# A fused retention and gated-MLP kernel: the last 64 rows of both sequences of a pair as one last block, one set of transposed mixing weights, bias rows by DMA

## The chip, the cores and the metric

The kernel runs on one core of one Trainium2 chip. The metric is the time of one execution in device microseconds. The granted clock is the clock that TensorE was given, as a share of its full speed. A run is called slow when it is over 1.5% above the fastest of the same kernel; ratios are taken over fast runs.

## The reference

Eight sequences of 576 rows go through eight heads of retention and then through a gated MLP whose gate mixes rows with a 576 x 576 matrix. Cut to what matters:

```python
# q, k, v: (8, 8, 576, 64) float32
scores = q @ k.transpose(0, 1, 3, 2) / sqrt(64)
Dmat   = where(rel >= 0, gamma[:, None, None] ** rel, 0)      # rel = row - column, one gamma per head
x      = heads side by side of (scores * Dmat) @ v            # (8, 576, 512)

h      = gelu_tanh(x @ w_in)                                  # w_in 512 x 1024
u, v   = h[..., :512], h[..., 512:]
v_n    = (v - mean(v)) / sqrt(var(v) + 1e-6) * g_ln
v_s    = einsum('ts,bsd->btd', w_sg, v_n) + b_sg[None, :, None]   # "token mixing", w_sg 576 x 576
out    = x + (u * v_s) @ w_out                                # float32, (8, 576, 512)
```

## The kernel before

The sequences are taken in four pairs. A pair has 2 x 576 = 1152 rows, which are nine tiles of 128 rows, numbered 0 to 8. Retention works on five blocks of a pair: four full ones of 256 rows, and one half block of 128. The table `RB` names, for each block, its number of tiles, its first tile and the chunks of rows in it as (sequence, row).

```python
RB = [(2, 0, ((0, 0), (0, 128))), (2, 2, ((0, 256), (0, 384))),
      (1, MID, ((0, 512), (1, 0))),                           # MID = 4: the half block is the third
      (2, 5, ((1, 64), (1, 192))), (2, 7, ((1, 320), (1, 448)))]
```

So the middle tile holds rows 512 to 575 of sequence 0 and rows 0 to 63 of sequence 1. In this order the nine tiles are simply 1152 consecutive rows of the output, and each tile of 128 rows is stored as one plain matrix:

```python
outf = out.rearrange("b s d -> (b s) d")
def m_store(i):
    nc.sync.dma_start(outf[128 * i:128 * i + 128, :], cur.pop(("ob", i))[:])
```

Sequence 1 starts in the middle of a tile, so its mixing weights have to be cut at other rows than those of sequence 0. Each sequence has its own five transposed tiles of w_sg, ten in all, 50 transposes on TensorE. Small bias rows are placed into them, and into the tiles `vmid`, by ScalarE:

```python
wT = [[consts.tile([128, S], BF, name=f"wT{e}_{j}") for j in range(SB)] for e in range(2)]
def build_wT(e, j):
    c0 = (64 if e == 0 else 0) + 128 * j
    ...
    for t in range(SB):
        nc.tensor.transpose(tp[:, 128 * t:128 * t + 128], wnat[:, t, c0:c0 + 128], ident[:])
def place_vmid():
    for t in vmid:
        nc.scalar.activation(t[0][NB0:NB0 + 4, :], row4b[:, 0, :F2], Act.Copy)
        nc.scalar.activation(t[1][0:4, :], row4b[:, 0, :F2], Act.Copy)
```

An output tile is `op = uT @ w_out` in PSUM. For the first pair x is added by four more matmuls with the identity and ScalarE evicts; for later pairs a transposing transfer brings x into `xr`, and VectorE adds it at eviction:

```python
def m_X(i):
    ...
    nc.sync.dma_start_transpose(cur["xr", i][:], xTs[p][:, m].rearrange("p j r -> p (j r)"))
def m_Oev(i):
    ...
    if i // NT < XP:                                          # XP = 1: the first pair
        ins = nc.scalar.activation(ob[:], op[:], Act.Copy)
    else:
        ins = nc.vector.tensor_tensor(ob[:], op[:], cur.pop(("xr", i))[:]..., op=Alu.add)
```

For the last block of the last pair, q and k too are transposed by a transfer (`qkT<-qkb` from SBUF to SBUF), not on TensorE. In the profile lines, `pp` are PSUM tiles of the attention, `zd` the products for the retention states, `hv` and `hu` the two halves of x @ w_in, `wp` the token mixing, `op` the output tiles, `qkT` transposed q and k, `xr` transposed x.

All loads, stores and transposing transfers are issued by SyncE into one queue, in the order of a table `ORDER`. The same table holds dummy matmuls (`f9`, `f11`: products into a scratch tile `scr`) that fill gaps of TensorE in the first 45 us.

## Time and profile before

| | kernel before |
|---|---|
| median of 3 runs | 212.21 us (212.01 to 212.43) |
| span of the profiled run, granted clock | 209.1 us, 1.00 |
| TensorE busy | 94% |
| 128x512 output stores (256 KB each) | 36, each of 128 rows of 2 KB |

Here are three further lines of the kernel before: the shares of the chain of work that ended last (fourth part of the page), and, for the line that issues the output stores, the issue times and the time from issue to landing.

```profile
PE 58%; DMA 11%; POOL 9%; SPq 8%; DVE 7%; ACT 3%; issue 2%; DVEq 0%; POOLq 0%; ACTq 0%
```

### The profile page before, as it was taken

What the parts mean: (1) busy time and instruction counts of PE and PEld (TensorE: products, weight loads), DVE (VectorE), ACT (ScalarE), POOL (GpSimd) and SP (SyncE); (2) the same over time, 40 slices, a digit from 0 to 9 for tenths busy, and PEclk for the clock granted to TensorE, in tenths of its full rate; (3) what the DMA queues carried; (4) which work ended last, traced back from release to release, by engine and by line L of the source; (5) the groups of instructions that cost most, each with busy time, mean ns of one, the idle gap of its engine ahead of it and who ended that gap; (6) DMA issues with size and microseconds to landing.
All of it is one profiled execution on the core that took longest, in us unless ns stands there. A gap on an engine that the chain in (4) does not pass through costs nothing.

```text
span 209.1 us, 7861 instructions
## 1 busy us (share of the span) xinstructions
PE 196.8 (94%) x3378; PEld 130.9 (63%) x3378; DVE 152.7 (73%) x293; ACT 119.1 (57%) x198; POOL 113.1 (54%) x157
## 2 busy tenths in 40 slices
PE   7998769999999999999999999999899999999982
PEld 3555456577666768765876676658476657566750
DVE  6876668779949768973994966998677886567463
ACT  3216898894984864469656527575526484534300
POOL 5390369696578788656688498165196070112000
PEclk9999999999999999999999999999999999999999
DMA  6999999999999999999999999998778977255565
GB/s 169 290 334 206 336 262 346 297 298 250 195 270 290 260 261 242 258 252 315 290 264 257 304 264 181 217 213 202 199 205 180 226 107 127 102 154 149 155 201 176
DMA packets 94117, 48.64 MB, mean 233 GB/s; under 512 B 38202, under 2 KB 87362, under 8 KB 94082
## 3 DMA queue, kind: packets, MB, share of 16 engines
q1 hardware_dynamic: 94064, 48.13, 96.5%
q8 instruction: 26, 0.43, 0.9%
q14 instruction: 9, 0.07, 0.2%
q10 hardware_dynamic: 18, 0.00, 0.0%
HBM read 32.79 MB, written 9.44 MB: 202 GB/s over the span
## 4 chain that ended last, share of the span: by engine, by line
PE 58%; DMA 11%; POOL 9%; SPq 8%; DVE 7%; ACT 3%; issue 2%; DVEq 0%; POOLq 0%; ACTq 0%
PE wp L759 15%; PE op L786 10%; PE hv L693 10%; PE hu L740 8%; PE pp L626 5%; DMA uT<-in_moe_w_in_dram 4%; SPq L431 3%; POOL vb L463 3%; POOL qkb L463 3%; PE pp L543 3%; DMA qkT<-qkb 3%; DMA ld<-in_q_dram 2%; PE pp L503 2%; DVE bst L708 2%; DMA xr<-xT 2%
## 5 line engine op out<-in xcount | busy, mean ns | idle before, releaser
L463 POOL TENSOR_TENSOR qkb<-ld,gqv 128x1024 bf16<-128x1024 f32 (+1 forms) x19 | 32.7, 1721 | 22.0 <-DMA ld<-in_q_dram 13.2
L556 DVE TENSOR_TENSOR ret<-pp,msk 128x1024 bf16<-128x1024 f32 x32 | 38.6, 1219 | 5.8 <-PE pp L543 5.5
L759 PE MATMUL wp<-wT,vn 128*128 128x288 bf16 x256 | 40.3, 286 | 0.0
L463 POOL TENSOR_TENSOR vb<-ld,gqv 128x1024 bf16<-128x1024 f32 (+1 forms) x20 | 34.4, 1730 | 8.1 <-DMA ld<-in_v_dram 8.0
L740 PE MATMUL hu<-xT,w_in 128*128 128x256 bf16 (+1 forms) x320 | 37.0, 262 | 1.9 <-ACT xT L682 1.9
L682 ACT ACTIVATE xT<-pp 128x512 bf16<-128x512 f32 (+1 forms) x40 | 24.8, 671 | 23.3 <-PE pp L626 21.5
L693 PE MATMUL hv<-w_in,xT 128*128 128x512 bf16 x144 | 36.2, 380 | 1.6 <-DVE w_in L371 0.9
L769 DVE TENSOR_TENSOR uT<-wp,uT 128x288 bf16<-128x288 f32 x64 | 27.2, 448 | 11.5 <-PE wp L759 11.3
L786 PE MATMUL op<-w_out,uT 128*128 128x512 bf16 x144 | 34.9, 380 | 0.7 <-DVE uT L769 0.6
L708 DVE BATCH_NORM_STATS2 bst<-vg 128x6 f32<-128x512 f32 x36 | 24.7, 685 | 12.1 <-ACT vg L700 12.1
L740 PEld LDWEIGHTS <-w_in 128*128 128x128 bf16 x320 | 27.9, 98 | 8.8 <-issue 2.1
L700 ACT ACTIVATE vg<-hv 128x512 f32<-128x512 f32 x36 | 21.2, 596 | 16.5 <-PE hv L693 11.8
L759 PEld LDWEIGHTS <-vn 128*128 128x128 bf16 x256 | 24.8, 98 | 8.1
L728 ACT ACTIVATE vn<-vg,mv 128x512 bf16<-128x512 f32 x32 | 25.4, 809 | 6.7 <-POOL mv L716 6.6
L750 ACT ACTIVATE uT<-hu 128x512 bf16<-128x512 f32 x36 | 20.9, 595 | 11.4 <-PE hu L740 11.1
L713 POOL TENSOR_SCALAR mv<-mv 128x2 f32<-128x2 f32 (+1 forms) x20 | 4.5, 224 | 41.0 <-DVE mv L709 40.4
L693 PEld LDWEIGHTS <-xT 128*128 128x128 bf16 x144 | 13.2, 98 | 14.2 <-ACT xT L682 1.6
L786 PEld LDWEIGHTS <-uT 128*128 128x128 bf16 x144 | 13.3, 98 | 13.8 <-DVE uT L769 1.0
L802 DVE TENSOR_TENSOR ob<-op,xr 128x512 f32<-128x512 f32 x27 | 17.9, 687 | 5.1 <-PE op L786 5.0
L512 DVE COPY qkT<-pp 128x2048 bf16<-128x2048 bf16 (+1 forms) x15 | 16.6, 1108 | 4.0 <-PE pp L503 4.0
L457 POOL CAST qkb<-ld 128x1024 bf16<-128x1024 f32 (+1 forms) x19 | 18.0, 945 | 2.4 <-DMA ld<-in_k_dram 2.4
L759 PE MATMUL wp<-wT,vmid 128*128 128x288 bf16 x64 | 17.9, 287 | 0.0
(89 smaller groups left out, 234.6 us busy)
## 6 DMA issues: line engine op xcount, KB each, us to landing
out_dram<-ob SPq DMA_DIRECT2D x36, 256.0 KB, 3.6
ld<-in_q_dram SPq DMA_DIRECT2D x16, 512.0 KB, 7.3
ld<-in_k_dram SPq DMA_DIRECT2D x16, 512.0 KB, 6.3
ld<-in_v_dram SPq DMA_DIRECT2D x16, 512.0 KB, 7.1
wst<-in_moe_w_sg_dram SPq DMA_DIRECT2D x2, 576.0 KB, 7.1
wst<-in_moe_w_in_dram SPq DMA_DIRECT2D x1, 1024.0 KB
ld<-in_k_dram SPq DMA_DIRECT2D x8, 128.0 KB, 6.9
ld<-in_q_dram SPq DMA_DIRECT2D x8, 128.0 KB, 6.9
```

The source lines that it names most:

```text
L463: eng.tensor_tensor(dst, src, g.unsqueeze(3).to_broadcast(list(src.shape)), op=Alu.mult)
L556: ins = nc.vector.tensor_tensor(ret[:].rearrange("p r (k t) -> p (r k) t", k=2), sc[:].rearrange("p r (k t) -> p (r k) t", k=2), msk2[:].r ...
L682: nc.scalar.activation(dst, src, Act.Copy)
L693: ins = nc.tensor.matmul(hv[:], xTs[p][:, m, kk, :], w_in[:, kk, F2:], start=(kk == 0), stop=(kk == KK - 1))
L700: unfence(nc.scalar.activation(vgs[i][:], cur.pop(("hv", i))[:], Act.Gelu_apprx_tanh), ("V", i))
L708: nc.vector.bn_stats(bst[:], vgs[i][:])
L728: nc.scalar.activation(vn[:], vg[:], Act.Identity, scale=mv[:, s, 2:3], bias=mv[:, s, 3:4])
L740: ins = nc.tensor.matmul(hu[:, n, :], w_in[:, kk, 128 * c:128 * c + 128], xTs[p][:, m:m + w, kk, :], start=(kk == 0), stop=(kk == KK - 1), ...
L750: unfence(nc.scalar.activation(uTs[p][:, c0:c1, 128 * m:128 * m + 128 * w], cur.pop(("hu", i, half))[:], Act.Gelu_apprx_tanh), ("U", i, half))
L759: ins = nc.tensor.matmul(ps[:], vns[t0 + j][e][:, 128 * c:128 * c + 128], wT[e][j][:, half * HS:(half + 1) * HS], start=(j == 0), stop=(j ...
L769: ins = nc.vector.tensor_tensor(uTs[p][:, c, col:col + HS], cur.pop(("wp", b, c, half))[:], uTs[p][:, c, col:col + HS], op=Alu.mult)
L786: ins = nc.tensor.matmul(op[:], uTs[p][:, c, r], w_out[:, c, :], start=(p >= XP and c == 0), stop=(c == KK - 1), skip_group_check=True)
```

## The change

The intent is to do one thing once instead of twice. If both sequences of a pair are cut at the same rows, they can share one set of mixing weights. The last 64 rows of *both* sequences then form the half block, which comes last in the pair, and all token mixing of the pair follows it. Cuts are marked with "..."; the new order of jobs is left out.

```diff
 RB = [(2, 0, ((0, 0), (0, 128))), (2, 2, ((0, 256), (0, 384))),
-      (1, MID, ((0, 512), (1, 0))),
-      (2, 5, ((1, 64), (1, 192))), (2, 7, ((1, 320), (1, 448)))]
+      (2, 5, ((1, 0), (1, 128))), (2, 7, ((1, 256), (1, 384))),
+      (1, MID, ((0, 512), (1, 512)))]
-XP = 1
+XT = 9
+LAST = NP * NT - 1
...
-wT = [[consts.tile([128, S], BF, name=f"wT{e}_{j}") for j in range(SB)] for e in range(2)]
+wT = [consts.tile([128, S + 64], BF, name=f"wT{j}") for j in range(SB - 1)]
+wS = [consts.tile([128, S], BF, name=f"wS{e}") for e in range(2)]
...
 def m_W(b, c, half):
     for j in range(SB):
+        w_ = wS[e][:] if t0 + j == NT * p + MID else wT[j - e][:, :S] if e else wT[j][:, 64:]
         ins = nc.tensor.matmul(ps[:], vns[t0 + j][e][:, 128 * c:128 * c + 128],
-                               wT[e][j][:, half * HS:(half + 1) * HS],
+                               w_[:, half * HS:(half + 1) * HS],
...
 def m_store(i):
-    nc.sync.dma_start(outf[128 * i:128 * i + 128, :], cur.pop(("ob", i))[:])
+    nc.sync.dma_start(out_rows(i), cur.pop(("ob", i))[:])
+
+def out_rows(i):
+    p, m = divmod(i, NT)
+    if m == MID:
+        return out[2 * p:2 * p + 2, 512:S, :]
+    r0 = (2 * p + (m > MID)) * S + 128 * (m - (MID + 1) * (m > MID))
+    return outf[r0:r0 + 128, :]
...
-def place_vmid():                                  # six copies on ScalarE
-    ...
-def build_wT(e, j):
+def place(dst, a, c0, c1):                         # seven small transfers
+    nc.sync.dma_start(dst, row4b[:, a, c0:c1])
+def build_wT(j):
...
-ZC = ((0, 1), (0, 1), (1,), (0, 1), (0,))          # states: now both halves of each full block
...
+def m_Oh(i, hf):                                   # the last tile (i == LAST) in two halves of 256 columns
+    ...
```

Besides this, the first k cast moves from ScalarE to VectorE, as does one eviction of x, and buffers change (`zb` 4 to 5, `zs` 3 to 2, `vn` 10 to 13).

## The prediction

> **What bounds the kernel now.** I read the page first (busy shares, the slices), then the chain of waits, the busy times of three stretches, and the timelines of ScalarE at the start and of all engines at the end.
>
> ```profile
> PE 196.8 (94%) x3378; PEld 130.9 (63%) x3378; DVE 152.7 (73%) x293; ACT 119.1 (57%) x198; POOL 113.1 (54%) x157
> PE   7998769999999999999999999999899999999982
> ACT  3216898894984864469656527575526484534300
> DMA  6999999999999999999999999998778977255565
> ```
>
> TensorE is nearly full from slice 8 (about 40 us) to slice 38; DMA is full over the first 27 slices (146 us). The 94% flatters the start: the warm-up matmuls on a dummy tile (the scr group) take 14.5 us there. The stretches are start, dense part and tail:
>
> ```profile
> 0.00:39.50 39.50, 33.06 (x586) 19.70 (x587) 27.93 (x64) 23.60 (x38) 22.50 (x39) 1.00 1.05 279
> 39.50:205.35 165.85, 163.72 (x2795) 111.16 (x2794) 124.07 (x229) 95.53 (x161) 90.63 (x119) 1.00 0.97 222
> 205.35:209.10 3.75, 0.00 (x0) 0.00 (x0) 0.69 (x1) 0.00 (x0) 0.00 (x0) 1.00 0.51 194
> ```
>
> The third column is TensorE's busy time. In the dense part it is idle for 165.85 - 163.72 = 2.1 us, so that part costs what TensorE has to do. I sum the jobs of the program with durations from the chain of waits: a mixing job (5 matmuls wp) 0.61 us, an output tile (4 op) 0.86, four hv 0.86, eight hu 0.87 to 0.89, 32 attention transposes 0.57, 5 transposes of w_sg 0.28, 32 zd about 0.27. The whole program holds about 170.6 us of such work (warm-up left out), 16.0 of it issued before 39.5 us, 154.6 after. The remaining 165.85 - 154.6 - 2.1 = 9.2 us I put on the 59 changes between jobs on 64x64 tiles and jobs on the full array: 0.16 us each (an estimate, a remainder).
>
> So three things set the end: how much useful work is done by 40 us, the total of TensorE work plus changes, and the tail. At the start the limits are transfers and ScalarE's order:
>
> ```profile
> 18.88 1.06 ACT L373 ACTIVATE w_in<-wst 128x1024 bf16<-128x1024 f32 x1 [0.67 <-DMA wst<-in_moe_w_in_dram]
> ...
> 22.98 0.63 ACT L856 ACTIVATE vmid<-row4b 4x512 bf16<-4x512 bf16 x1
> 24.11 1.06 ACT L373 ACTIVATE w_in<-uT 128x1024 bf16<-128x1024 f32 x1 [0.50 <-DMA uT<-in_moe_w_in_dram]
> 25.18 1.28 ACT L700 ACT_TABLE_LOAD   x1
> 26.48 0.60 ACT L700 ACTIVATE vg<-hv 128x512 f32<-128x512 f32 x1
> ```
>
> The first hv matmuls end at 21.5 us, their gelu starts at 26.48: four placements of bias rows (2.5 us), a weight cast that waits for its load, and a table load stand ahead of it.
>
> **What the Trainium skill says.** "TensorE: Matmul & The Clock Gate", section "Back-to-back issue gap", gives N / 2.4 + 2.5 ns per warm matmul: 55.8 ns for 128 columns, 122.5 for 288, 215.8 for 512. The trace agrees: 0.28 us for 5 transposes, 0.61 for 5 wp, 0.86 for 4 op. The columns of the groups (219, 286, 380 ns) are latencies and must not be multiplied by counts. The same page, section "Architectural detail", says that ScalarE and VectorE are strict FIFO; the gelu stuck behind the cast shows it. "Trainium Kernel Development and Optimization", section "Performance Expectations", calls matmul busy time a bad metric; here 14.5 us of it is dummy work, which is why I count jobs instead.
>
> **The change, part by part.**
>
> 1. Six tiles of w_sg for ten: 25 transposes fewer on TensorE, 25 x 56 ns = -1.4 us, on the path. VectorE saves about 0.7 us of copies, off the path (73% busy).
> 2. States: every full block now makes both halves and the half block none: 512 zd matmuls for 480, +32 x 8 ns = +0.27 us. The half block multiplies its state by 64 columns in place of 128 in part: about -0.2 us.
> 3. Order of jobs: after the point where 16 us of work is issued, the new order has 54 changes of array mode where the old one has 59: -5 x 0.16 = -0.8 us.
> 4. ScalarE loses the six placements of bias rows (4 x 0.63 + 2 x 0.68 = 3.9 us), the first k cast (1.06) and one x eviction (0.74). The rows go by seven small transfers, k and the eviction to VectorE. In the new order the table load and two gelus stand ahead of the second w_in cast, so the first gelu should start near 21.5 us, five earlier.
> 5. Loads: the third block is a full one (1.57 MB for 0.79), and the w_sg load moves behind block 5. I count bytes ahead of each load in the program's order and use what this trace moved: 4.9 MB by 21.4 us, then about 0.33 MB/us. The u half of w_in then lands near 27 us (24.1 before), the fourth block near 32, block 5 near 37, block 6 near 44, the half block near 48, w_sg near 52. Token mixing, which filled TensorE from 46.7 us, starts much later (37 us of work are ahead of it); the work in its place is attention and hv/hu of blocks 3 to 6. With 5 us on GpSimd per block (1.90 + 1.03 + 1.90) and some 5 more until its last job, the loads allow about 22 us of work by 42 us, 27 by 47, 33 by 54: just above what a dense TensorE would use. The last dummy matmuls stand at 12.8 us of useful work in place of 16.0. I place that at about 34 us, so 16.0 is reached near 37.9 us in place of 39.5: -1.6 us.
> 6. The end. In the last pair all 16 mixing jobs and 9 output tiles (16 x 0.61 + 9 x 0.86 = 17.6 us of pure TensorE work) come after the last norm. That adds no work, it only moves it. Before:
>
> ```profile
> 202.03 0.46 DVE L769 TENSOR_TENSOR uT<-wp,uT 128x288 bf16<-128x288 f32 x1 [0.15 <-PE wp L759]
> 202.54 2.27 PEld L786 LDWEIGHTS <-uT 128*128 128x128 bf16 x12 [0.86 <-DVE uT L769]
> ...
> 205.35 0.69 DVE L802 TENSOR_TENSOR ob<-op,xr 128x512 f32<-128x512 f32 x1 [0.17 <-PE op L786]
> ```
>
> TensorE waits 0.55 us for the last gate before its last three tiles. The new order has five tiles there, and the first need not wait. The last tile is cut in two: its last eviction is 256 wide (about 0.42 us for 0.69) and its store 128 KB, not 256 KB; the old store took 209.1 - 206.04 = 3.06 us, and I give the half one 0.5 us less. Together -1.4 us.
>
> Sum: -1.4 + 0.1 - 0.8 - 1.6 - 1.4 = -5.1 us. I give back 0.5 us for idle time in the middle, as TensorE will run closer to its loads. 212.2 - 4.6 = 207.6 us, 2.2% less.
>
> **The rivals.** (a) Loads or GpSimd become the limit between 40 and 60 us: token mixing no longer fills TensorE, and DMA is already at nine tenths. For it: margins of one or two us in part 5; against it: the half block's 256-byte rows and 1.2 MB of w_sg are out of the early queue. It would cost 2 to 3 us and leave 210 to 211. (b) The start gains more: with ScalarE free early, TensorE has three whole blocks (16.5 us of work) where it had two and a half, and 16.0 us could be reached by 36 us; that makes 205 to 206. (c) VectorE limits the end: 16 gates of 0.45 and 9 evictions of 0.69 are 13.4 us in 17.6 of TensorE, with stores and nine transposing transfers beside them. Then the end gain turns into waits of the last tiles for their transposed x: 209. (d) Nothing moves because the early work is DMA-bound anyway and only parts 1 and 3 count: 210.
>
> **Range and chances.** The certain parts (work, mode changes, tail) make about -3 us, the start -3 to +2, the middle and end 0 to +2. 204.5 to 211.3 us should hold it. The 2% line lies at 207.97, beside my centre: 0.53 faster, 0.43 same, 0.04 slower.
>
> **What would show it right or wrong.** Right: first gelu before 23 us; TensorE dense from about 35 us on; 25 w_sg transposes of 0.28 us per five; no gate wait before the last tiles; less than 3.3 us between the last matmul and the end. Wrong: TensorE idle, waiting for GpSimd or loads, between 40 and 60 us (rival a), waits of the last tiles for VectorE or for the transposed x (c), or a dense part whose length does not follow the job count, which would mean that my 0.16 us per mode change is not that.

## More of the kernel before

```profile
L806 SPq DMA_DIRECT2D out_dram<-ob x36: 332/530/2348, 65.2 to 206.1; - x36
...
DMA to landing us min/median/max: 2.0/3.6/6.3
```

The chain stands on TensorE for over half of the span and on transfers for a ninth of it. A store lands 3.6 us after its issue in the median, and never more than 6.3 us.

## The result

Ratios are the mean time of one kernel's fast runs over the mean time of the other's fast runs of the same rounds, so not quite the ratio of the medians quoted.

| | before | after |
|---|---|---|
| median | 212.11 us, 4 runs (211.68 to 212.43) | 235.0 us, 4 runs (232.83 to 236.07) |
| ratio of fast runs | 1 | 1.1068, interval 1.0984 to 1.1152 |
| span of the profiled run, granted clock | 209.1 us, 1.00 | 231.1 us, 0.972 |

The changed kernel is slower by about 11%. First its page: busy times, four rows of the 40 slices of 5.8 us, and the shares of the chain that ended last.

```profile
PE 197.6 (86%) x3357; PEld 131.5 (57%) x3389; DVE 155.2 (67%) x296; ACT 113.2 (49%) x190; POOL 113.9 (49%) x157
...
PE   7899769998999998999799989999971999977920
...
ACT  2007657998972656577275664754550166700000
...
PEclk9999999999999999999999999999998599999995
DMA  6999999999997999989999999999998136796595
...
PE 46%; DMA 23%; SPq 13%; DVE 8%; issue 4%; POOL 3%; ACT 2%; DVEq 0%; POOLq 0%; ACTq 0%
```

TensorE is busy for 197.6 us, nearly as before (196.8): the work has not grown, the span has. The hole in its row in the 31st slice, which begins at 173.3 us (the 1, after a 7), the two 7s from 202.2 us and the 2 near the end are new. Transfers show a hole in the next slices, where the DMA row falls to 1 and 3. The share of transfers in the chain has doubled, from 11% to 23%.

What did transfers do in such a hole? The view of the transfers from 169 to 177 us of the changed kernel has slices of 0.2 us. A digit is the mean busy share of the 16 DMA engines in tenths; below it is what they moved. A packet counts in the slice in which it starts, with its whole time and size, so the view tells what begins in a slice.

```profile
DMA  2011112022899999911130011111111199999970
GB/s 20 10 10 44 32 45 52 4 64 54 188 224 216 116 68 55 52 51 51 51 51 0 10 41 61 41 61 41 61 41 54 32 200 289 349 273 242 37 3 0
```

From 172.4 to 175.4 us the digit is 1, but for three slices near 173.2, and from 172 us on some 51 GB/s are moved. Two of 16 engines are 0.125, a 1 in this row. When it ends, 200 to 349 GB/s come at once: something had been waiting. The trace's packets say what it was:

```
stretch at the store of    us                longest 256-byte packet in it, us
pair 0                      96.38-100.29      3.88
pair 1                     171.55-175.48      3.89
pair 2                     201.97-205.51      3.24
pair 3                     220.66-225.25      4.49
kernel before: longest 256-byte packet of the whole run 1.79 us
```

The loads of the half blocks have 256-byte rows too, but in each stretch a transposing transfer is the first or second thing that SyncE issued behind the store, and the standing packets (17, 17, 5 and 5 of over 1 us) are put down to it. In these stretches only some twelve packets of 2 KB start per 0.5 us, while the small packets stand, and for some 3 us no new one starts. Packets of a plain store behind the one of pair 2 stood as well, up to 3.53 us.

The waits that this causes are in the list of waits of the changed kernel (engine, tile and line, what was waited for: us in total, times, longest), and in its timelines, where the bracket gives the idle time before and its releaser.

```profile
DVE ob L805 <- DMA xr<-xT: 14.7, 4, 6.9
...
PE pp L558 <- DMA qkT<-qkb: 6.2, 1, 6.2
```

```profile
178.20 0.43 PE L558 MATMUL pp<-qkT 64*64 64x64 bf16 x16 [6.25 <-DMA qkT<-qkb]
...
226.02 1.89 DVE L805 TENSOR_TENSOR ob<-op,xr 128x512 f32<-128x512 f32 x3 [6.93 <-DMA xr<-xT]
```

TensorE stands for 6.25 us before the scores of the last half block, since their transposed q and k are late, and its clock is 0.8 in that slice of the page and 0.5 in the next. At the end VectorE stands for 6.93 us for transposed x. For the line of the stores the landing times are now:

```profile
L832 SPq DMA_DIRECT2D out_dram<-ob x35: 332/574/3036, 78.4 to 227.9; - x35
...
DMA to landing us min/median/max: 2.1/2.3/8.0
```

The median store is *faster* than before (2.3 us, not 3.6), and only the longest is slower (8.0, not 6.3). A mean or a median of the stores would have hidden the four bad ones.

**The theory** is then: the 2 x 64 x 512 store is served by two DMA engines, at 64 rows of 2 KB each, and transfers that are spread over all engines, the transposing ones above all, must wait until those two are free. The Trainium skill's page "DMA: Bandwidth & Descriptors", section "Why a DMA increments its semaphore by 16 and not by 1", says that the number of engines is the largest number up to 16 that divides the slowest dimension (other than 1) of both access patterns; here that is 2, and for the other 31 whole-tile stores, of 128 rows, 16. The kept traces can settle this number. They hold the times at which the semaphore that tells of a store's landing is raised, and for the middle tiles of three kernels (the last two are runs of experiments 1 and 3) these are:

```
form of one store     semaphore raised                         issue to last rise, us
2 x 64 x 512          once about 1 us after issue, then 2      7.6 to 8.2
4 x 16 x 512          once about 1 us after issue, then 4      4.0 to 5.6
64 x 512              16 times                                 2.3 to 4.4
```

That is what two, four and sixteen engines would report, each at the end of its share, apart from the one early rise of the first two forms. The same page's section "Queues, rings and completion order" says that on each engine descriptors are consumed in ring order. That would hold up whatever stands behind the store on its two engines. Why no 256-byte packet starts on the other fourteen either is not shown, as the packets of the trace do not name their engine. **Rivals** are the ones of the prediction: the loads and bias-row transfers of the start, the order of jobs itself, and the tail with its waits for transposed x.

### The profile page after: what moved, and what is told of

Same layout as the page of the kernel before. It is cut to its first block, busy times and chain, and to the rows that moved or that the text cites. A ratio compares the mean times of both kernels' runs of the same rounds, so it can differ in the third digit from the quotient of the medians.

```text
span 231.1 us, 7862 instructions
## 1 busy us (share of the span) xinstructions
PE 197.6 (86%) x3357; PEld 131.5 (57%) x3389; DVE 155.2 (67%) x296; ACT 113.2 (49%) x190; POOL 113.9 (49%) x157
## 4 chain that ended last, share of the span: by engine, by line
PE 46%; DMA 23%; SPq 13%; DVE 8%; issue 4%; POOL 3%; ACT 2%; DVEq 0%; POOLq 0%; ACTq 0%
PE wp L763 10%; PE hv L696 9%; PE hu L743 9%; PE op L789 8%; SPq L434 8%; DMA ld<-in_k_dram 7%; DMA xr<-xT 6%; DMA qkT<-qkb 4%; PE pp L626 4%; DMA ld<-in_q_dram 3%; DMA out_dram<-ob 2%; PE pp L558 2%; DVE ret L571 2%; SPq L798 2%; SPq L367 1%
## 5 line engine op out<-in xcount | busy, mean ns | idle before, releaser
L696 PE MATMUL hv<-w_in,xT 128*128 128x512 bf16 x126 | 35.7, 389 | 2.1 <-ACT xT L685 1.1
L711 DVE BATCH_NORM_STATS2 bst<-vg 128x6 f32<-128x512 f32 x36 | 24.7, 686 | 16.0 <-ACT vg L703 15.8
L789 PE MATMUL op<-w_out,uT 128*128 128x512 bf16 x126 | 34.1, 387 | 0.8 <-issue 0.2
L685 ACT ACTIVATE xT<-pp 128x512 bf16<-128x512 f32 (+1 forms) x39 | 24.1, 671 | 21.0 <-PE pp L626 20.3
L743 PEld LDWEIGHTS <-w_in 128*128 128x128 bf16 x320 | 28.6, 99 | 7.6 <-issue 1.6
L558 PE MATMUL pp<-qkT 64*64 64x128 bf16 (+1 forms) x576 | 13.2, 218 | 8.4 <-DMA qkT<-qkb 6.2
L763 PE MATMUL wp<-wS,vmid 128*128 128x288 bf16 x64 | 17.5, 286 | 2.9 <-DVE ob L805 2.9
```

What stands on the lines that cost most here:

```text
L685: nc.scalar.activation(dst, src, Act.Copy)
L696: ins = nc.tensor.matmul(hv[:], xTs[p][:, m, kk, :], w_in[:, kk, F2:], start=(kk == 0), stop=(kk == KK - 1))
L711: nc.vector.bn_stats(bst[:], vgs[i][:])
L743: ins = nc.tensor.matmul(hu[:, n, :], w_in[:, kk, 128 * c:128 * c + 128], xTs[p][:, m:m + w, kk, :], start=(kk == 0), stop=(kk == KK - 1), ...
L763: ins = nc.tensor.matmul(ps[:], vns[t0 + j][e][:, 128 * c:128 * c + 128], w_[:, half * HS:(half + 1) * HS], start=(j == 0), stop=(j == SB ...
L789: ins = nc.tensor.matmul(op[:], uTs[p][:, c, 128 * m:128 * m + 128], w_out[:, c, :], start=(i >= XT and c == 0), stop=(c == KK - 1), skip_ ...
```

## The experiments

Sixteen kernels were run. All results are correct where not said otherwise.

### 1. The middle tile stored as two stores of 64 rows

```diff
 def m_store(i):
-    nc.sync.dma_start(out_rows(i), cur.pop(("ob", i))[:])
+    ob = cur.pop(("ob", i)); p, m = divmod(i, NT)
+    if m == MID:
+        for e in range(2):
+            nc.sync.dma_start(out[2 * p + e, 512:S, :], ob[64 * e:64 * e + 64, :])
+    else:
+        nc.sync.dma_start(out_rows(i), ob[:])
```

> The changed kernel, with the store of the middle tile (2x64x512, four of them) issued as two stores of 64 rows. Theory (the two-part store runs on two DMA engines and everything behind it waits there): the long packets of 3 to 5 us at four places vanish, 2048-byte packets come at the usual rate, and the time falls from 235 to 205 to 211 us. Rival (too many transposing transfers and stores crowd the end since both token mixings lie there): 225 us or more, the waits for xr stay. Rival (small transfers of bias rows): no change, 233 to 236 us.

Measured: 216.79 us (214.99 to 217.15, 4 runs), ratio to the kernel before 1.0235 (1.0166 to 1.0303). From 235.0 us this is 18.2 us less, with the same bytes and one more instruction per pair. That is above the 205 to 211 us expected: the theory held for the largest part of the loss, not for all. Its row of TensorE, the one wait for transposed q and k, and the last two lines of VectorE:

```profile
PE   7999798979999999999999999999999699999970
```

```profile
170.43 0.32 PE L558 MATMUL pp<-qkT 64*64 64x64 bf16 x16 [1.94 <-DMA qkT<-qkb]
...
209.49 1.29 DVE L805 TENSOR_TENSOR ob<-op,xr 128x512 f32<-128x512 f32 x2 [2.31 <-DMA xr<-xT]
...
211.65 0.69 DVE L805 TENSOR_TENSOR ob<-op,xr 128x512 f32<-128x512 f32 x1 [0.88 <-DMA xr<-xT]
```

The waits of 6.25 and 6.93 us have become 1.94 and 2.31. The 1 near 173 us is now a 6, and the two 7s after 202 us are gone.

### 2. The same form of store put into the kernel before

The kernel before gets the two-part store for its own middle tile; the rows land in the wrong places. So that no row is written twice, the last tile of each pair goes out as two plain halves, the form that experiment 1 uses.

```diff
+    if m == MID:
+        nc.sync.dma_start(out[2 * p:2 * p + 2, 512:S, :], ob[:])
+    elif m == NT - 1:
+        nc.sync.dma_start(out[2 * p + 1, 448:512, :], ob[:64, :])
+        nc.sync.dma_start(out[2 * p + 1, 0:64, :], ob[64:, :])
+    else:
+        nc.sync.dma_start(outf[128 * i:128 * i + 128, :], ob[:])
```

> The kernel before, with only the store of the middle tile in the two-part form 2x64x512 (rows of the output permuted, a wrong result on purpose; the last tile of a pair is stored as two halves of 64 rows so that no row is written twice). Theory: four stores on two engines stop the queue some 6 us each and the time rises from 212 to between 220 and 235 us. Rivals (end crowded, bias rows, order of jobs): 212 to 214 us.

Measured: 230.86 us (229.6 to 233.77), ratio 1.0897 (1.0821 to 1.0974). Nothing else of the change is in this kernel (the plain halves beside it land 2.3 to 5.6 us after their issue in its trace), and yet it is 19 us slower than without. Its view of the transfers from 215 to 223 us, and the last line of VectorE in its timeline:

```profile
DMA  5699687969999292299990111111111149999980
GB/s 113 215 225 155 114 151 123 149 129 192 170 117 128 74 52 77 47 46 32 23 44 20 51 51 51 51 51 51 51 51 41 42 74 264 289 214 366 451 338 10
```

```profile
222.48 1.29 DVE L802 TENSOR_TENSOR ob<-op,xr 128x512 f32<-128x512 f32 x2 [5.69 <-DMA xr<-xT]
```

The same row of ones, the same 51 GB/s, the same wait for transposed x. So the form of the store costs about as much in either kernel, whatever the order of jobs. That is the first half of the answer, shown in both directions.

### 3. A store in four parts

If the number of parts sets the number of engines, a store in parts of four must cost about half. Rows are permuted (wrong), so that the store keeps its four parts and cannot be read as one plain matrix.

```diff
-            nc.sync.dma_start(out[2 * p + e, 512:S, :], ob[64 * e:64 * e + 64, :])
+            nc.sync.dma_start(out[2 * p + e, 512:S, :].rearrange("(s g) f -> g s f", g=4), ob[64 * e:64 * e + 64, :])
```

> The kernel with two half-sequence stores, each of them now written in a form of 4 x 16 x 512 (the rows permuted, so the result is wrong on purpose). If the number of parts in the slowest dimension sets how many engines carry a store, each engine gets 16 rows of each of two stores, 32 rows of 2 KB, half of the 64 rows that an engine got in the changed kernel: the stall halves, to 2 to 2.5 us per store, and of the 18.2 us between the changed kernel (235.0) and this one with plain halves (216.8) about 7 to 10 return: 224 to 227 us. If any three-dimensional form were slow for another reason, it would be near 235; if only the spanning of two sequences were at fault, near 217.

Measured: 224.07 us (223.25 to 226.36), ratio 1.0621 (1.0526 to 1.0717). Between the ratios of plain halves (1.0235) and of two parts (1.1068) this is (1.0621 - 1.0235) / (1.1068 - 1.0235) = 46% of the loss. The two waits, from its timeline:

```profile
173.90 0.32 PE L558 MATMUL pp<-qkT 64*64 64x64 bf16 x16 [3.28 <-DMA qkT<-qkb]
...
216.30 1.29 DVE L805 TENSOR_TENSOR ob<-op,xr 128x512 f32<-128x512 f32 x2 [4.67 <-DMA xr<-xT]
```

Both lie between those of the plain halves and of two parts. A general slowness of three-dimensional stores, or of stores that span two sequences, is out. One detail was expected otherwise: instead of standing for 2 to 2.5 us, no 256-byte packet near these four stores took over 1.41 us. The small packets start more slowly while the stores run, so the loss halves by another course than the expectation named.

### 4. One two-part store alone, of the first or of the last pair

Both are the kernel of experiment 1 with one pair left in the old form: `if m == MID and p > 0` and `if m == MID and p < NP - 1`.

> As a_two_stores, but the middle store of the first pair alone stays in the two-part form (near 93 us). Theory: the queue stops just as long there, but TensorE has loaded blocks and mixing work to do: 1 to 4 us more than a_two_stores, less than a_slow_last. Rivals: the same time as a_two_stores.

> As a_two_stores, but the middle store of the last pair alone stays in the two-part form. Theory: the end waits for the transposed x and the last stores behind it, 5 to 8 us more than a_two_stores. Rivals: the same time as a_two_stores.

Measured: first pair 218.75 us (218.58 to 219.9), ratio 1.0356 (1.03 to 1.0413); last pair 220.07 us (218.13 to 222.28), ratio 1.0354 (1.0261 to 1.0446). By the ratios one such store costs 1.2% of 212, some 2.5 us, at either end; the intervals touch or overlap that of experiment 1 (1.0166 to 1.0303), so the size is uncertain. The first pair fell into the 1 to 4 us expected, the last missed its 5 to 8. Four times 2.5 is 10 us and not 18, so either the stores of the middle pairs cost more or the costs do not simply add. One of the middle ones, pair 1's at 171.55 us, is the one that holds up the transposed q and k of the last half block; that it alone carries the rest was not tried.

### 5. Without the seven bias-row transfers

`place` does nothing. Its output is wrong, which doesn't matter for the time.

> As a_two_stores, but the seven small transfers that place the bias rows are left out (a wrong result on purpose). Theory (4.1 us of the queue's issue time between 54 and 61 us, but the loads that TensorE then waits for are issued before): under 1 us, 216 to 217.5. Rival (they hold up the loads and explain the work lost between 40 and 60 us): 2 to 3 us less, 214 to 215.

Measured: 219.62 us (217.32 to 220.46), ratio 1.0335 (1.0281 to 1.0389). There is no saving; the rival that the small transfers cost time falls. By the ratios the kernel is even 1% slower than with them, though the intervals overlap a little. An edit that only takes transfers away should not do that; experiments 7 and 8 look at what such edits move.

### 6. The tail and the last half block

In the first kernel the last three plain tiles of the order (29, 33, 34) take x by identity matmuls, as the first pair does, and ScalarE evicts them. In the second, q and k of the last half block are transposed on TensorE instead of by a transfer. The third has both. All start from experiment 1.

```diff
+TAIL = (29, 33, 34)
...
-    if i < XT:
+    if i < XT or i in TAIL:          # m_O and m_Oev; m_X returns at once for these tiles
```

> As a_two_stores, but the last three output tiles (by order: 33, 34, 29) take x through TensorE's identity matmuls and are evicted by ScalarE, in place of a transposing transfer and VectorE. Theory (with two stores the end still waits, 2.3 and 0.9 us, for the last transposed x, which stand behind stores in the one queue): those waits go, TensorE has 12 matmuls of 56 ns more (0.7 us), the time falls by 1.5 to 3 us from a_two_stores (216.8), to about 214.5. Rival (the end is bound by the stores alone): no change, 216 to 218 us.

> As a_two_stores, but the last block (the half one) is transposed on TensorE and evicted by VectorE in place of a transposing transfer. Theory (the last block stands alone at the end of the attention, its load and its transposing transfer are bare: TensorE waits 1.9 us for it at 170 us and runs the next 4 us at half clock): 2 to 4 us less than a_two_stores, 213 to 215. Rival (its load is what is late, not the transposing transfer): under 1 us.

> a_tail and a_last_t together. If both waits are in series on the chain that ends last, the gains add: 210.5 to 213 us, equal to or just under the kernel before (211.9). If they overlap: 213 to 215.

Measured: tail, fast runs 213.6, 214.0 and 216.41 us (three slow ones 217.21 to 219.3), ratio 1.0125 (1.0063 to 1.0187); last half block 216.53 us (215.21 to 218.2), ratio 1.0208 (1.0163 to 1.0253), which is not told from experiment 1; both, 215.44 us (212.91 to 219.96), ratio 1.0131 (1.0081 to 1.0181). So the waits for transposed x at the end were worth about 1% (the interval just overlaps that of experiment 1). Transposing the last half block elsewhere brought nothing by itself, and the 2 to 4 us expected did not come. The expectation's rival, that the load is what is late, fits the traces. In experiment 1 GpSimd already waits for q of that block, before anything is transposed:

```profile
161.49 1.05 POOL L466 TENSOR_TENSOR qkb<-ld,gqv 128x512 bf16<-128x512 f32 x1 [3.20 <-DMA ld<-in_q_dram]
```

With the transpose on TensorE this wait is 3.24 us, and TensorE then stands 1.19 us for GpSimd's cast of k in place of the 1.94 us for the transfer.

### 7. Pauses of TensorE without a wait

After experiment 1 TensorE still stands between 40 and 60 us, where the kernel before is full. The main pause of the kernel of experiment 1 in that stretch is this one ("issue" is time in which no wait is recorded):

```profile
44.70 0.44 PE L589 MATMUL zd<-vb,qkb 64*64 64x64 bf16 x30 [1.36 <-issue]
```

In six kernels with the new order such pauses stood before the same records of TensorE, 1460 or 1969 or both, counted over matmuls and weight loads; the changed kernel itself has one of 0.5 us before 1969, and the one with only the first store slow has neither. The traces also show 26 transfers of 16 KB in a queue named "instruction" (6746 records of TensorE in 26 transfers are 259 each, if all of them are TensorE's); one of them had ended 1.4 us before the pause's end. Two theories: the pause belongs to a place in the stream of instructions, or to the job (a hidden wait of these zd matmuls). Moving all later instructions on, without a change of jobs, tells them apart. The first attempts cut the first one or two groups of dummy matmuls into pieces 64 wide:

> The kernel with two half-sequence stores, with its first group of warm-up products cut into pieces 64 wide, the same columns in all, so that every later TensorE instruction stands some 60 places further on in the stream of instructions; no job, order or data changes. In four of the earlier runs TensorE stood still for 1.0 to 1.4 us before instruction 1460 of its records (at 43 to 45 us), in four runs before 1969 (near 57 us), in several before 4945, with no wait in the records, each just after a 16 KB transfer[...]. If these pauses belong to places in the stream (fetching), the pause near 44 us falls on a job some 60 instructions earlier in the program and keeps a place near 1460, or goes. If they belong to the job (a hidden wait of the 32 zd matmuls), the pause stays before the third zd matmul of that same job, now at place 1520 or so. Time under both: 215 to 218 us.

> As the run before, with the first two groups cut, so that later instructions stand some 120 places further on. Under fetching the pauses are again at places near 1460 and 1969 of the records or have moved[...], so on jobs some 120 instructions earlier; under a wait of the job they keep their jobs. Time under both: 215 to 218 us.

Measured: 225.08 us (ratio 1.0591, 1.0495 to 1.0686) and 222.68 us (1.0541, 1.0458 to 1.0624). The expectation of an unchanged time failed: the small pieces took 7.94 us where the wide ones had taken 4.21, and TensorE began its first useful job 4.8 and 8.5 us later. The zd pause was gone in both, but their times are no fair test. (The pauses without a wait of the first one stood before records 955 and 1211.) The second attempt replaces one 512-wide product in each of the first two groups by twelve small ones (32 x 64) of about the same time together:

```diff
+            if cur["fills"] <= 2:
+                parts = parts[:-2] + [(32, 64)] * 12 + parts[-1:]
```

> The kernel with two half-sequence stores, with one 512-wide warm-up product in each of the first two groups replaced by twelve small ones (32 x 64), about as long together: later TensorE instructions stand some 90 records further on, at nearly the same time (the earlier attempt cost 4 us of TensorE time at the start). If pauses of TensorE with no wait in the records belong to places in the instruction stream, the pause of 1.36 us before the third zd product at 44 us leaves that job and pauses fall on other jobs, 250 or 500 records apart, each about 1 us after the end of a 16 KB instruction transfer. If it belongs to the job it stays there. Time: 215 to 218.5 us under both; by the first theory it may differ by up to 2 us, as pauses fall in better or worse places.

Measured: 219.71 us (219.51 to 221.77), ratio 1.0352 (1.0299 to 1.0405), so 1.2% slower than experiment 1 with the same jobs in the same order. From its timeline:

```profile
43.13 0.83 PE L747 MATMUL hu<-xT,w_in 128*128 128x256 bf16 x6 [1.51 <-issue]
...
55.41 0.29 PE L518 MATMUL pp<-ident,qkb 64*128 64x64 bf16 x8 [1.59 <-issue]
```

The pauses now stand before hu matmuls and before attention transposes, and no longer before zd. By count of records they are at 1461 and 1969, where they were. Places in the stream, then, not jobs. Useful work done by 60 us is 28.7 us in this kernel and 32.1 in that of experiment 1. The pauses are 1.7 us of this 3.4 (1.51 + 1.59 - 1.36). As much again goes with the granted clock, which was 0.57 from 56 to 60 us, right after the second pause, and 1.00 in experiment 1; the 6 in the clock row of its page:

```profile
PEclk9999999999699999999999999999999999999998
```

Whether the pause brought the clock down is not shown. The same shift on the tail version:

> The kernel with two half-sequence stores and the last three plain tiles taking x by matmuls (213.6 to 216.4 us in fast runs) with the same small shift of the instruction stream. In its trace it lost 2.15 us in a pause before record 1969, at 55.65 us. If pauses belong to places in the stream, that pause leaves its job, and the time is 212 to 216; if they belong to jobs it stays.

Measured: 217.91 us, but three of four runs were slow ones (the fast one 212.78). Its pauses, read in a slow run, stood at 1461 and 1969 as well.

### 8. Without the later dummy matmuls

The dummies after the third group are left out, in the kernel of experiment 1 and in the kernel before; then together with the tail of experiment 6.

```diff
+            cur["fills"] = cur.get("fills", 0) + 1
             for w in [512] * (n // 4) + [128 * (n % 4)] * (n % 4 > 0):
+                if cur["fills"] > 3:
+                    break
                 nc.tensor.matmul(scr[:, :w], warm[:, :128], warm[:, :w], ...)
```

> The kernel with two half-sequence stores, without the warm-up products after the third group (4.13 us at 12.7, 1.35 at 19.3, 0.5 at 24.7 and 1.12 at 34.0 us of its trace). If dummy work stands in front of useful work in the first 40 us, which would be where the predicted gain of 1.6 us at the start went, 16 us of useful work are done before 38 us in place of 39.0, and the time falls by 1 to 2 us. If they only fill time in which TensorE waits for data, the curve of useful work keeps its times and the time stays within 1 us, or grows if the clock falls.

> The kernel before without its warm-up products after the third group (about 7 us of TensorE time after 11 us). If leaving them out helps either kernel alike, the time falls by about 1% to 210 us, and then the gain says nothing of the change. If the gain in the new order came from pauses and one transfer wait that this kernel does not have, it stays within 0.5% of 212, or grows a little as the clock is lower early on.

> Both changes that gained something over two half-sequence stores: the last three plain tiles take x by matmuls (1.0235 to 1.0125 of the kernel before), and the warm-up products after the third group are left out (1.0235 to 1.0138). If they act in different places (the tail; the pauses and the transfer wait at 168 to 172 us), they add up: 1.0125 x 1.0138 / 1.0235 = 1.003, about 212.5 us, the same as the kernel before within 2%. If the gain of the second was only luck of where pauses fall, it stays at 1.01 or above.

Measured: new order 215.4 us (214.02 to 216.06), ratio 1.0138 (1.01 to 1.0176); kernel before 216.21 us (214.19 to 217.8), ratio 1.021 (1.0163 to 1.0258); new order with tail 214.56 us (212.31 to 217.1), ratio 1.0076 (1.0019 to 1.0133).

The first theory of these runs, that dummies had stood in front of useful work at the start, falls: without them 16.0 us of useful work are done by 40 us, with them 16.7. The gain lies later. Useful work of TensorE done by a time, counted from the traces (each weight load times its share of the job's duration):

| us done by | before | two stores (exp. 1) | few dummies | changed kernel | before, few dummies |
|---|---|---|---|---|---|
| 40 us | 16.7 | 16.7 | 16.0 | 15.8 | 16.9 |
| 60 us | 34.7 | 32.1 | 32.4 | 31.6 | 32.4 |
| 165 us | 135.1 | 133.1 | 133.0 | 130.0 | 131.6 |
| 175 us | 145.1 | 139.3 | 142.2 | 136.0 | 141.4 |

The kernel before became slower by 2%, which neither case of its expectation had (210 us, or within about 0.5% of 212), and the interval of the new order just overlaps that of experiment 1. With few dummies the new order lost 3 us less between 165 and 175 us. The wait for transposed q and k there is 0.41 us, where it was 1.94 in experiment 1 (the bracket):

```profile
168.97 0.32 PE L561 MATMUL pp<-qkT 64*64 64x64 bf16 x16 [0.41 <-DMA qkT<-qkb]
```

The kernel before answers in the other direction. Without its later dummies a pause of the same kind appears where it had none; from the timeline of that kernel, and then the busy times of TensorE (third column) between 40 and 60 us, first of that kernel and then of the kernel before:

```profile
42.43 0.41 PE L546 MATMUL pp<-qkT 64*64 64x128 bf16 x14 [1.68 <-issue]
```

```profile
40.00:60.00 20.00, 17.29 (x346) 12.59 (x349) 15.68 (x31) 14.76 (x25) 12.23 (x15) 1.00 1.17 262
```

```profile
40.00:60.00 20.00, 19.81 (x411) 14.52 (x410) 16.67 (x32) 15.83 (x26) 13.46 (x18) 1.00 1.12 249
```

So the kernel before lost 2.5 us of TensorE in a stretch that the missing dummies do not touch. The new pause stands before record 1208, which is 253 before 1461 and 255 after 953. What changed is where its instructions stood, and its clock and times early on; which of these made the pause was not tried apart. It seems that the kernel before runs well in its first 60 us because it was tuned there, and that an edit of its instructions can lose this. No version here beats the kernel before; the best, with two stores, the tail and few dummies, is 0.8% slower.

## Why the prediction was wrong

The prediction was 207.6 us, the result 235.0: the direction was wrong, and 27.4 us are to be told.

**The failed step is a term that its sum does not have.** The prediction added up parts, "-1.4 + 0.1 - 0.8 - 1.6 - 1.4 = -5.1 us", and no part asks what the store of the middle tile becomes. Of the end it said "That adds no work, it only moves it", and the one store that it reckoned with, that of the last tile, it priced by bytes ("128 KB, not 256 KB"). The bytes of the middle tile's store are the same as before; the form is not. The store went from 128 x 512 to 2 x 64 x 512, and with that from 16 engines to two. Experiment 1 takes 18.2 us away by undoing this alone, experiment 2 puts 19 us into the old kernel by doing this alone, and experiment 3 finds 46% at twice the engines. The shape stood in the diff, in `out_rows`, before anything was run.

**The remaining 9 us** are 4.6 us of forecast gain that did not come and some 4.6 us of loss against the kernel before. Spans of the profiled runs place the loss (6.3 us in the run profiled): the kernel of experiment 1 has its last plain matmul at 209.3 us, before 205.35 (3.9 later), and ends 6.1 us after it, before 3.75 (2.4 more). By the prediction's own steps:

1. *Fewer transposes, states, mode changes (parts 1 to 3).* The counts came as told: 25 transposes of w_sg for 50, 512 zd for 480, and mode changes from the point of 16 us of useful work on, counted in the traces, are 53 for 57 (54 for 59 told). By the prediction's count the work fell from 170.6 to 169.4 us. This step holds; 0.16 us per mode change stays an estimate, as no run isolates it.
2. *ScalarE (part 4).* "The first gelu should start near 21.5 us": 22.4 us. The mechanism was right, and it bought nothing, as the next step shows.
3. *Loads and start (part 5).* The loads came about when told: the second weight half cast at 26.8 us (27 told), the fourth block's transposes at 33.2 (its load told near 32), the last dummies at 34.0 (34 told). But "16.0 is reached near 37.9 us" did not follow: counted in one way for both, it is 39.0 us in experiment 1 and 38.0 before. The term of -1.6 us measured +1.0; by this count most of it was never there, since the 39.5 us that it started from should have been 38.0. Experiment 8 shows that dummies in the way are not the reason.
4. *Rival (a), "loads or GpSimd become the limit between 40 and 60 us".* Useful work was lost there, 2.6 us in experiment 1 by the table, near the 2 to 3 us named, but not to such waits: of TensorE's 2.46 us of idle time there 1.36 are the pause without a wait, and its longest recorded wait is 0.36 us, for ScalarE. Experiment 7 ties such pauses to places in the instruction stream, and experiment 8 makes one in the old kernel. That they are the fetching of instructions is argued from the 16 KB transfers that end 1.3 to 1.6 us before each pause ends; it is not shown. Nor is the pause all of it: the changed kernel has one of 0.5 us there and still loses 2.2 us, the one with few dummies has none and loses 1.6. What takes these stays open.
5. *165 to 175 us.* The prediction looked at no wait here, yet 3.8 us were lost (2.0 us behind before it, 5.8 after). The transposed q and k of the last half block come late, 1.94 us, and TensorE's mean clock from 160 to 200 us is 0.96. Experiment 6 says that transposing elsewhere does not mend it, as the block's load is late already (GpSimd waits 3.2 us for it), experiment 8 that the loss shrinks when what lies before it moves. The same load is waited for there, 2.93 us, so its cause stays open beyond that.
6. *The end (part 6).* "-1.4 us" became +2.4. The tile that is cut in two is not the last in the order: tiles 33, 34 and 29 follow it, so no last eviction of 256 columns and no half store ends the program; and a wait of 0.45 us for VectorE's gate (u times the mixed v) is still there. Rival (c), "the end gain turns into waits of the last tiles for their transposed x", is what happened, at 2.31 and 0.88 us. Experiment 6 takes these waits away and gains 1.1%, 2.3 us.

One reading of the prediction was also off without effect: the 27 full slices of DMA end at 141 us, not 146.

Points 3 to 6 tell where the 9 us are. That they add up exactly is not shown: the effects of pauses and waits shift one another, as experiments 5 and 8 make plain.

## What to carry to other kernels

When a change moves rows, write down for every transfer not only its bytes but the shape that the instruction carries, and look at its outermost dimension; two or four there can cost more than all the arithmetic that the change saves, and two plain transfers are the cure. Look at the longest landing and the DMA row next to a wait, not at the median, and suspect a low, flat busy share (here a row of ones at 51 GB/s) of being a few engines at work; here the rises of the store's semaphore, 2, 4 or 16 at its end, told how many. In a kernel with thousands of small TensorE instructions, differences of 1% between versions can come, it seems, from where instructions stand in the stream, so undo a part in more than one way before believing a gain or a loss of that size.

## What the Trainium skill lacked or had wrong

- "DMA: Bandwidth & Descriptors" has the rule for the number of engines, and its section "Rules for kernel authors" the advice on an outermost dimension below 16. It gives no price for others: here a 256 KB store on two engines held 256-byte packets of transposing transfers for 3.2 to 4.5 us at the longest, and four of them made 18 us of 212.
- The same page does not say that one transfer of few engines is seen in a profile as a low and flat busy share: 1 in tenths of 16 engines, 51 GB/s, as against 200 to 349 GB/s right after.
- No page gives pauses of TensorE that come back at the same records of its stream, here 0.5 to 2.4 us each, some 254 records or a multiple of that apart (953, 1208, 1461, 1969), in versions whose times differ by 1 to 2%. If they are the fetching of instructions, which is not shown, the point belongs to "Runtime: NRT & Kernel Launch".
